# A recorded order from a table of ranks, and a dense layer that waits chunk by chunk

## Chip, cores, metric

One core of one Trainium2 chip. The metric is the device time of one execution in microseconds (us), lower is better. The profiled span, from the core's first to its last instruction, is some 1.7 us shorter than the device time; numbers called "span" are from the trace, the others are device times.

## What is computed

Two layers, each run twice: an attention with memory (32 heads of width 20, four segments of 512 rows) and a dense layer with relu, both on a normalised input with a residual. Cut to what matters:

```python
def _A_ref(x, wq, wk, wv, wo, beta):            # x: 1 x 2048 x 640, bf16
    ...                                          # q, k, v: 32 heads of 20, 4 segments of 512
    for s in range(N):
        logits = jnp.einsum('bhqd,bhkd->bhqk', qs, ks) * scale + mask     # causal inside a segment
        p = _softmax(logits, axis=-1)
        a_dot = jnp.einsum('bhqk,bhkd->bhqd', p, vs)
        num = jnp.einsum('bhld,bhde->bhle', pq, M)                        # read of the memory
        ...
        outs.append(g * a_mem + (1.0 - g) * a_dot)
        M = M + jnp.einsum('bhld,bhle->bhde', pk, vs)                     # write of the memory
        ...
    return o @ wo

def _B_ref(x, w1, w2):                           # 640 -> 1728 -> 640
    h = jnp.maximum(jnp.einsum('bsd,df->bsf', x, w1), 0)
    return jnp.einsum('bsf,fd->bsd', h, w2)

x = A_x
x = x + _A_ref(_layernorm(x), A_wq, A_wk, A_wv, A_wo, A_beta)
x = x + _B_ref(_layernorm(x), B_w1, B_w2)
x = x + _A_ref(_layernorm(x), A_wq, A_wk, A_wv, A_wo, A_beta)
x = x + _B_ref(_layernorm(x), B_w1, B_w2)
```

## The kernel before

The kernel is not written down in its final order. It is a set of generators (scores, products with the values, projections, normalisations, dense layers), each of which yields steps; a scheduler with a clock of its own (a guess of each step's duration) picks step after step and records it on its engine with the waits it needs. The hardware then runs each engine's instructions in that order. Which of several possible steps is recorded next:

```python
# Sched.run, cut: for each step that could be recorded now
b = self._best(op, None if st.first else resv)
end, start, k, rank = b            # rank: earliest start by the scheduler's own clock
key = (round(rank), op.due, st.serial)
if best is None or key < best[0]:
    best = (key, st, end, start, k)
```

`op.due` is the part that can be steered: without a table it comes from a rough pacing of the generators, and with one from `dues[key]`. Before, the table came out of 14 plans, each handing the next one the latest starts that would still end on time, and then 29 recorded random changes:

```python
for n in range(PLANS):              # 14
    P, S = plan(dues)
    end = max(S.t.values())
    new = justify(S)                # latest start of each step that keeps the end
    ...
end, P, S, dues = best
for seed in MOVES:                  # 29 seeds
    dues = shake(S, dues, seed)
    P, S = plan(dues)
```

The score rounds (L1286) write two double accumulator banks, X and Y, which two exponentials on ScalarE (L1300, L1297) empty; a triangular mask on Pool (L1276) follows. All other matmuls but the products with the values share three banks, MISC. The dense layer's first half makes 14 chunks of relu (13 of 128 features at L1586, a last one of 64 in another tile mode at L1598), the second half (L1616) sums over them:

```python
S.spawn(relu(NFULL, bk, tk), "relu")
w2t = yield Need("w2")
hr = []
for dc in range(NFULL + 1):         # all 14 chunks are asked for here
    th = yield Need("h", b, s, dc)
    hr.append(th)
for i in range(NJ):
    for hf in range(2):
        bk = None
        for dc in range(NFULL + 1):
            ...                      # fn: one 320-column matmul of chunk dc
            if dc == 0:
                _, bk = yield pe(mm_ns(320), lambda bank, fn=fn: [(lambda e: fn(e, bank), False)],
                                 (hr + w2t if i == hf == 0 else []), [MISC])
            else:
                tk = yield pe(mm_ns(320), lambda fn=fn, bank=bk.ap, dc=dc: [
                    (lambda e: fn(e, bank), dc == NFULL)])
```

The softmax here doesn't subtract the row's maximum and nothing guards it: scores larger than these inputs give would overflow.

## Time and profile before

| | before |
|---|---|
| device time, median (range) of 3 | 575.22 us (574.92 to 575.4) |
| span of the profile, granted TensorE clock | 573.2 us, 1.0 |
| first matmul; last matmul start to end | 1.25; 3.1 us |
| streaming of the matmuls | 500.5 us |
| 399 changes of tile mode | 38.6 us |
| small gaps, under 8 ns; 8 to 30 ns | 6.6; 6.5 us |
| stalls of 30 ns or more in the first 10 us | 3.5 us |
| later stalls: ahead of score rounds; relu ahead of the second half; all others | 3.76; 1.10; 8.30 us |

The page's busy share (97%) says that TensorE is the bound, but not how much an order could give. The table does: it is made from the start times of all matmuls, each gap between two starts minus the streaming time of the first. Only the last row, 13.2 us, is something that an order can take away, since it neither removes a matmul nor, as the prediction counts, a change of mode. The last row is sorted by the matmul that starts after the stall. Two matmul records are missing from this trace (5112 matmuls, 5114 weight loads).

### The profile page before, as it was taken

Reading aid. Unit: us, or ns where it says so; the run is one execution under the profiler, and the core shown is the slowest. Engines: PE = TensorE matmul, PEld = TensorE weight load, DVE = VectorE, ACT = ScalarE, POOL = GpSimd, SP = SyncE. Lnnn points to the kernel's source line nnn. Section 1 sums busy time; section 2 is a strip of 40 time slices with the busy share of each in tenths; the row PEclk is TensorE's granted clock in tenths of the full one; section 3 lists DMA queues with packets and bytes.
Section 4 is the critical chain, followed back from the end, with each engine's and each line's share of the span. In section 5 each row is a group of like instructions: output and inputs, shape, how many; then the busy total and the mean of one; then the engine's idle time right before and its main releaser. Section 6 shows DMA issues by size and latency. Waiting matters only on the chain.

```text
span 573.2 us, 12504 instructions
## 1 busy us (share of the span) xinstructions
PE 558.8 (97%) x5112; PEld 297.3 (52%) x5114; DVE 425.0 (74%) x1023; ACT 424.5 (74%) x517; POOL 213.3 (37%) x342
## 2 busy tenths in 40 slices
PE   8999989999999999999999999999999999999998
PEld 4454545444564444655446544455445644755655
DVE  6699989988999968976789683699756897624202
ACT  4899898989879978779998787896785887022140
POOL 3474546654444433444434441344331333002000
PEclk9999999999999999999999999999999999999999
DMA  6256777487354625545163720455315921522101
GB/s 217 94 126 137 148 137 150 145 217 108 66 79 71 94 43 87 95 74 106 31 123 58 115 50 15 71 97 89 66 19 69 160 55 19 92 64 44 50 0 47
DMA packets 126609, 50.62 MB, mean 88 GB/s; under 512 B 112120, under 2 KB 124600, under 8 KB 126552
## 3 DMA queue, kind: packets, MB, share of 16 engines
q1 hardware_dynamic: 124568, 42.19, 40.1%
q0 software_dynamic: 1552, 7.29, 4.3%
q8 instruction: 40, 0.66, 0.5%
q10 hardware_dynamic: 432, 0.34, 0.2%
q14 instruction: 17, 0.14, 0.1%
HBM read 15.16 MB, written 7.37 MB: 39 GB/s over the span
## 4 chain that ended last, share of the span: by engine, by line
PE 72%; DVE 20%; ACT 4%; DMA 2%; issue 1%; POOL 1%; SPq 0%; DVEq 0%
PE ps L1586 17%; PE ps L1616 17%; PE ps L947 12%; PE ps L1286 6%; PE ps L994 6%; PE ps L1532 5%; PE ps L1368 5%; ACT PT L1300 2%; DVE x_sb L1474 2%; DVE phq L1206 1%; DVE hT L1567 1%; DMA wv_r<-in_A_wv_dram 1%; DVE xn_tok L877 1%; DVE o_sb L1420 1%; DVE ktok L1142 1%; DVE stats L865 1%
## 5 line engine op out<-in xcount | busy, mean ns | idle before, releaser
L1300 ACT ACTIVATE PT<-ps 128x1024 bf16<-128x1024 f32 x256 | 248.2, 1024 | 38.5 <-PE ps L1286 37.7
L1276 POOL TENSOR_SCALAR_AFFINE_SELECT PT<-PT 128x512 bf16<-128x512 bf16 x256 | 171.0, 686 | 256.1 <-ACT PT L1300 220.5
L1616 PE MATMUL ps<-wb,hT 128*128 128x320 bf16 x896 | 133.7, 299 | 1.6 <-ACT hT L1568 1.0
L1586 PE MATMUL ps<-xnT,wb 128*128 128x512 bf16 x520 | 126.8, 380 | 1.0 <-DVE o_sb L1225 0.6
L1474 DVE TENSOR_TENSOR x_sb<-x_sb,ps 128x320 bf16<-128x320 bf16 x128 | 60.6, 478 | 68.5 <-PE ps L1616 54.8
L1616 PEld LDWEIGHTS ps<-wb,hT 128*128 128x128 bf16 x896 | 84.2, 98 | 38.7 <-issue 4.9
L1568 ACT ACTIVATE hT<-ps 128x512 bf16<-128x512 f32 (+1 forms) x64 | 36.8, 576 | 56.2 <-PE ps L1586 54.8
L1586 PEld LDWEIGHTS ps<-xnT,wb 128*128 128x128 bf16 x520 | 47.1, 98 | 56.5 <-issue 6.2
L1297 ACT ACTIVATE PT<-ps 128x1024 bf16<-128x1024 f32 x64 | 62.4, 1028 | 12.3 <-PE ps L1286 12.3
L994 PE MATMUL ps<-wv_r,xnT 128*128 128x320 bf16 x320 | 57.5, 300 | 1.1 <-DMA wv_r<-in_A_wv_dram 0.5
L947 PE MATMUL ps<-xnT,wq_p 128*128 128x512 bf16 x200 | 54.8, 380 | 0.4 <-DVE o_sb L1451 0.2
L947 PE MATMUL ps<-xnT,wk_p 128*128 128x512 bf16 x200 | 53.9, 380 | 0.0
L1532 PE MATMUL ps<-wo_r,oT 128*128 128x320 bf16 x280 | 47.4, 300 | 0.2 <-DVE x_sb L1474 0.2
L1368 PE MATMUL ps<-PT,va 128*32 128x128 bf16 (+3 forms) x896 | 40.7, 302 | 0.0
L994 PEld LDWEIGHTS ps<-wv_r,xnT 128*128 128x128 bf16 x320 | 29.4, 98 | 20.4 <-issue 3.7
L1286 PE MATMUL ps<-kq 20*128 20x512 bf16 (+3 forms) x560 | 35.3, 301 | 2.1 <-ACT PT L1300 2.0
L1567 DVE TENSOR_SCALAR hT<-ps 128x512 bf16<-128x512 f32 (+1 forms) x48 | 32.0, 672 | 4.6 <-PE ps L1586 4.3
L877 DVE TENSOR_SCALAR xn_tok<-x_sb,mv,rstd 128x640 bf16<-128x640 bf16 x64 | 32.8, 522 | 3.4 <-POOL rstd L873 2.2
L1532 PEld LDWEIGHTS ps<-wo_r,oT 128*128 128x128 bf16 x280 | 25.7, 98 | 15.7 <-issue 3.6
L864 DVE BATCH_NORM_STATS2 stats<-x_sb 128x6 f32<-128x320 bf16 x64 | 29.8, 465 | 1.5 <-DMA x_sb<-in_A_x_dram 1.3
L865 DVE BATCH_NORM_STATS2 stats<-x_sb 128x6 f32<-128x320 bf16 x64 | 30.2, 472 | 0.0
L1368 PEld LDWEIGHTS ps<-PT,va 128*32 128x32 bf16 x896 | 18.9, 96 | 21.5 <-issue 9.2
(111 smaller groups left out, 625.3 us busy)
## 6 DMA issues: line engine op xcount, KB each, us to landing
kq_scr<-kq SPq DMA_DIRECT2D x28, 120.0 KB
kqL<-kq_scr SPq DMA_DIRECT2D x28, 120.0 KB
out_dram<-x_sb SPq DMA_DIRECT2D x16, 160.0 KB, 1.9
wb<-in_B_w_dram POOLq DMA_DIRECT2D x5, 432.0 KB, 4.0
x_sb<-in_A_x_dram POOLq DMA_DIRECT2D x3, 640.0 KB, 4.7
wb<-in_B_w_dram POOLq DMA_DIRECT2D x2, 640.0 KB, 6.0
kq_away<-hT SPq DMA_DIRECT2D x5, 256.0 KB, 2.3
kq<-kq_away SPq DMA_DIRECT2D x5, 256.0 KB, 3.5
```

The source lines that it names most:

```text
L877: tn, bx = yield dve(D, 4, lambda e, a, t=t: e.tensor_scalar(a, x_sb[:, t, :], mv[:, t, 0:1], rstd[:, t:t + 1], ALU.subtract, ALU.mult), [ ...
L947: fn = lambda e, bank, k=k, w_p=w_p, c=c: e.matmul(bank, w_p[:, k, c * 128:(c + 1) * 128], xnT[:, k_, :, k, :], start=(k == 0), stop=(k == ...
L994: fn = lambda e, bank, k=k, i=i, hf=hf: e.matmul(bank[:, 0:320], xnT[:, k_, i, k, :], wv_r[:, k, hf * 320:(hf + 1) * 320], start=(k == 0), ...
L1276: tm = yield pool(590.0, lambda e: e.affine_select(out=reg, in_=reg, pattern=[[0, 4], [1, 128]], compare_op=ALU.is_ge, fill=0.0, base=0, c ...
L1286: fns.append((lambda e, x=x, j=j, hh=hh, N=N, o=o: e.matmul(ps[:, hh, o:o + N], kq(b, gg[x], 0)[32 * hh:32 * hh + DH, 128 * j:128 * j + 12 ...
L1297: fn = lambda e: e.activation(PT[:, :, 2 * k:2 * k + 2, 1024:1280], bs.ap.rearrange("p h (x t) -> p x h t", x=2), ACT.Exp, scale=SCALE)
L1300: fn = lambda e: e.activation(PT[:, items[0], 2 * k:2 * k + 2, c0:c0 + 512], bs.ap, ACT.Exp, scale=SCALE)
L1368: return [(lambda e, hh=hh, j=j: e.matmul(bank[32 * hh:32 * hh + 32, 128 * j:L], v_flat[b][:, (j * H + 8 * hh + g) * E1:(j * H + 8 * hh + ...
L1474: ta = yield dve(320, 1, lambda e: e.tensor_tensor(xa, xa, bk.ap[:, 0:320], ALU.add), [tk], early=HOT)
L1532: fn = lambda e, bank, k=k, hf=hf, o=ot.ap: e.matmul(bank[:, 0:320], o[:, k, :], wo_r[:, k, hf * 320:(hf + 1) * 320], start=(k == 0), stop ...
L1586: fn = lambda e, bank, k=k, dc=dc: e.matmul(bank, w1_r[:, k, dc * 128:(dc + 1) * 128], xnT[:, k_, :, k, :], start=(k == 0), stop=(k == FC ...
L1616: fn = lambda e, bank, dc=dc, q=q, h=h, hf=hf: e.matmul(bank[:, 0:320], h, w2_r[:, q, hf * 320:(hf + 1) * 320], start=(dc == 0), stop=(dc ...
```

## The change

Two things. The 14 plans and 29 changes are replaced by one plan without a table and one with a table of ranks, shipped in the file, that a search found. And the dense layer's second half asks for a chunk only at the matmul that reads it: the first matmul waits for chunk 0, the next for chunk 1, and so on. The intent: fewer stalls of TensorE at the same work.

```diff
-PLANS = 14
-MOVES = (100008, 100014, 100017, ... )
-def justify(S): ...
-def shake(S, dues, seed): ...
+def ranked(S):
+    keys = sorted((l[7] for l in S.log if l[7]), key=lambda k: [(isinstance(x, str), x) for x in k])
+    step = array.array("h", zlib.decompress(base64.b85decode("".join(TABLE.split()))))
+    assert len(step) == len(keys)
+    return dict(zip(keys, itertools.accumulate(step)))
+TABLE = """ ... """                 # cut: the packed ranks, one for each step
...
                 w2t = yield Need("w2")
-                hr = []
-                for dc in range(NFULL + 1):
-                    th = yield Need("h", b, s, dc)
-                    hr.append(th)
                 for i in range(NJ):
                     for hf in range(2):
                         bk = None
                         for dc in range(NFULL + 1):
+                            hr = []
+                            if i == hf == 0:
+                                th = yield Need("h", b, s, dc)
+                                hr = [th]
...
-                                                 (hr + w2t if i == hf == 0 else []), [MISC])
+                                                 hr + w2t, [MISC])
                             else:
                                 tk = yield pe(mm_ns(320), lambda fn=fn, bank=bk.ap, dc=dc: [
-                                    (lambda e: fn(e, bank), dc == NFULL)])
+                                    (lambda e: fn(e, bank), dc == NFULL)], hr)
...
-        (the loop over PLANS and MOVES)
+        P, S = plan(None)
+        P, S = plan(ranked(S))
```

Most lines of the new kernel stand six lines higher: scores L1280, dense layer L1580, L1592 and L1610.

## The prediction

> **What bounds the kernel now.** I read the page first (busy shares, slices), then the stretches of the span with the busy time of each engine, then the waits of TensorE alone, then the instructions in order of time around the longest of those waits.
>
> ```profile
> PE 558.8 (97%) x5112; PEld 297.3 (52%) x5114; DVE 425.0 (74%) x1023; ACT 424.5 (74%) x517; POOL 213.3 (37%) x342
> PEclk9999999999999999999999999999999999999999
> ```
>
> TensorE is busy 558.8 of the span's 573.2 us and is never throttled. That leaves 14.4 us of idle time in which no matmul is in flight; no other engine is near its limit over the whole span. But busy time counts the modelled ends of pipelined matmuls, so I took the span apart by the start times of the 5112 matmuls instead:
>
> - First matmul at 1.25 us.
> - Streaming: a 512-column matmul starts a median 216 ns before its successor on the same line, a 320-column one 136 ns. With columns divided by 2.4 GHz per matmul (four row- or column-tiles counted once, 55 ns for the 128-column transposes, 39 ns for the 84-column ones) all streaming comes to 500.5 us.
> - Changes of tile mode: the scores are recorded in row tiles of 20x128, the products with the values in column tiles of 128x32, the last chunk of the dense layer in 128x64, everything else in 128x128. A 320-column matmul followed by a score round takes 232 ns start to start instead of 136; a 512-column score round followed by a full matmul 317 ns instead of about 213. So one change costs about 97 ns, and there are 399: 38.6 us.
> - Small excess: gaps under 8 ns over the streaming time add to 6.6 us, and 485 gaps of 8 to 30 ns to 6.5 us (about 13 ns each, which I read as the price of a wait that is already satisfied plus the small fixed cost).
> - Stalls of 30 ns or more: 52, 16.7 us together, of which 3.5 us lie before 9.9 us (cold warm-up matmuls, first normalisation, landing of the value weights). So 13.15 us of stalls are left for an order to remove.
> - Last matmul start to end of span: 3.1 us.
>
> Sum: 1.25 + 500.5 + 38.6 + 13.1 + 16.7 + 3.1 = 573.2.
>
> ```profile
> 60.00:115.00 55.00, 51.38 (x545) 25.74 (x544) 49.88 (x126) 51.09 (x60) 32.28 (x50) 1.00 0.68 145
> 200.00:300.00 100.00, 99.96 (x974) 50.43 (x974) 77.54 (x170) 85.77 (x100) 41.09 (x63) 1.00 0.45 79
> 485.00:573.00 88.00, 84.45 (x566) 51.84 (x564) 29.15 (x74) 18.71 (x33) 5.67 (x12) 1.00 0.22 48
> ```
>
> Columns: length, busy TensorE, weight loads, VectorE, ScalarE, Pool. Between 60 and 115 us TensorE, VectorE (91%) and ScalarE (93%) are all nearly full, and TensorE loses 3.6 us there; from 200 to 300 us it loses almost nothing; in the last stretch it is alone.
>
> ```profile
> PE ps L1286 <- ACT PT L1300: 2.5, 4, 1.4
> ...
> PE ps L1616 <- ACT hT L1568: 1.0, 2, 0.5
> ...
> PE ps L1616 <- DVE x_sb L1474: 0.6, 1, 0.6
> ```
>
> This view names the waits of TensorE (total us, count, longest). First the scores waiting for the exponentials that free their two double banks; then the second half of the dense layer (L1616) waiting for the relu of the first half; then a bank of the three shared ones waiting for VectorE.
>
> ```profile
> 81.63 0.39 PE L1286 MATMUL ps<-kq 20*128 20x512 bf16 x4
> 81.95 0.77 PE L1443 MATMUL ps<-ident,oraw 128*128 128x128 bf16 x8
> 82.09 1.95 ACT L1300 ACTIVATE PT<-ps 128x1024 bf16<-128x1024 f32 x2
> 84.09 0.40 PE L1286 MATMUL ps<-kq 20*128 20x384 bf16 x8 [1.37 <-ACT PT L1300]
> ...
> 553.81 0.74 PE L1598 MATMUL ps<-xnT,wb 128*64 128x256 bf16 x10
> 553.91 1.05 ACT L1568 ACTIVATE hT<-ps 128x512 bf16<-128x512 f32 x2 [0.48 <-PE ps L1586]
> 555.02 2.02 PEld L1616 LDWEIGHTS ps<-wb,hT 128*128 128x128 bf16 x16 [0.75 <-ACT hT L1568]
> 555.02 2.21 PE L1616 MATMUL ps<-wb,hT 128*128 128x320 bf16 x15 [0.48 <-ACT hT L1568]
> ```
>
> The order put only eight small transposes (0.77 us) between two score rounds, while the two exponentials of a round need 1.95 us: a stall. And at 555.02 the first matmul of the dense layer's second half waits until all 14 chunks of relu are done, though it reads only the first.
>
> **What the Trainium skill says.** "TensorE: Matmul & The Clock Gate", section "Wait — 56ns, not 53.3ns?", gives N / 2.4 GHz plus about 2.5 ns start to start for a warm stream; the 216 and 136 ns here agree. "TensorEngine Tiling (Array Packing)", section "Key Properties", says that a change of tiling mode drains TensorE; it gives no figure, the trace has about 97 ns. The first page, section "The mechanism" of its Part 3, has matmuls in strict order, only weight loads moving ahead: so a matmul at the head of the queue that waits for the relu holds back every later one, as at 555.02, and the recorded order is what counts. "Trainium Kernel Development and Optimization", section "Performance Expectations", warns that matmul busy time is a bad measure because matmuls are pipelined; this is why I counted starts.
>
> **The change, part by part.** Both orders were compared instruction by instruction.
>
> (a) The work is the same: 5114 matmuls before, 5113 after (one filling matmul less at the start), the same count of every line, the same exponentials. A few copies out of the accumulators move between VectorE (1025 to 1022 instructions) and ScalarE (522 to 524). Streaming stays 500.5 us: 0.
>
> (b) Changes of tile mode: 399 before, 400 after. At 97 ns: +0.1 us. The 38.6 us stay. I had hoped the search would save here; it does not.
>
> (c) Waits recorded on TensorE: matmuls with a wait 679 before, 691 after. At 13 ns: +0.2 us.
>
> (d) Chunk-wise wait. In the last two dense layers, where nothing else can be put between, the order after is the same as before, except that the waits now stand before the 1st, 13th and 14th matmul of the second half. Twelve matmuls of 136 ns, 1.63 us, now cover what was a stall of 552 ns each. The last relu ends about 0.55 us after the last matmul that feeds it, so both stalls go fully: 2 x 0.55 = -1.1 us. In the six other layers other matmuls stood there already and no relu stall is in the trace: 0.
>
> (e) Score rounds. I added up streaming and mode changes between the starts of successive score rounds (160 rounds). A round needs about 2.35 us (81.63 to 84.09 with other ScalarE work in the queue is 2.46; two exponentials alone are 1.95 plus the round itself and its handover). Sum of what is missing to 2.35 us per gap: before 3.5 us, with gaps of 0.86, 1.80, 1.88 and 1.99 us between the 24th and 34th; after 0.9 us, none under 2.08. The stalls on exponentials in the trace (1440, 602, 494, 480, 244, 217 and 143 ns) add to 3.6 us. So -2.6 us. The last round moves from 460 to 469 us of TensorE work: rounds are spread out more, so ScalarE and VectorE have more room in the crowded stretches.
>
> (f) The three shared accumulator banks. I counted groups that start less than 0.9 us after the end of the group three before them: 20 before, 12 after; under 1.0 us between 60 and 110 us of work: 8 before, 4 after. Stalls put down to these banks and to other VectorE work are what remains: 13.15 - 3.6 - 1.1 = 8.4 us. The counts fall by 40 to 50%; since only the search's own timing, not the chip, guarded the order, I take a third: -2.8 us.
>
> (g) Start and end: the first value matmul waits for its weights from memory (at 9.86 us before) in both orders; the last add and store are the same: 0.
>
> Sum: +0.1 + 0.2 - 1.1 - 2.6 - 2.8 = -6.2 us, from 575.2 to about 569.0. All of it lies on the path, since TensorE is the bound. I shade it to 568.5, because an order found by search was presumably kept for being good in ways my three counts do not see.
>
> **Rivals.** (1) The stalls only move: TensorE waits at the new places for VectorE, which is 91 to 93% busy between 60 and 200 us and gets no less work. For it: the old order was itself the best of 14 plans and 29 random changes, and its remaining stalls are largely where the chip differs from the recording's timing, which a new table would not know. Then only (d) and some of (e) stay: 572 to 574 us. (2) The search removes nearly all stalls: 13.15 us less and nothing added gives 562 us, just over 2%. For it: 160 rounds with no tight gaps; against it, mode changes and base are untouched, and some stalls come from transposing transfers (0.4 us at 176.7) that the order hardly rules. (3) The order is bad on the chip, a long transfer or a transposition late somewhere in the queue that issues them, with TensorE idle for 3 us and more: 580 us. Against it: DMA is at 68% at most in any of the stretches after 10 us, and SyncE has the same 217 instructions.
>
> **Range and chances.** A floor is 562 (no stall after 9.9 us); going more than 2% faster needs 563.7, so 11.5 of the 13.15 us. A ceiling with all gains lost is 575 to 576. Eight in ten: 564.5 to 572.5. Faster by over 2%: 0.06; within 2%: 0.92; slower: 0.02.
>
> **What would show it.** After: TensorE busy about 558 with idle time down from 14.4 to about 8 us; no wait of the second half (now L1610) on the relu, and the second half of the last two layers starting within 0.1 us of the chunk before it; scores waiting for exponentials under 1 us in total; 400 mode changes at the same 97 ns. I would be wrong if a mode change costs differently in another neighbourhood, if TensorE's waits for VectorE grow between 60 and 200 us, or if the first value matmul starts later than 9.9 us.

## The result, and the profile after

570.64 us (median of 4 runs, 569.9 to 571.42) against 575.12 us for the kernel before (4 runs, 574.92 to 575.4). The ratio is 0.9922, 95% interval 0.9905 to 0.9939: 0.8% faster, within 2%. All four runs of the new kernel were at clock 1.0. Ratios here and below are the mean time of one kernel's fast runs over that of the other's fast runs of the same rounds, so not quite the ratio of the medians quoted.

The busy line of the new kernel's page, and the first of the three stretches shown of before (length, then busy TensorE, weight loads, VectorE, ScalarE, Pool, then clock, DMA share, GB/s):

```profile
PE 558.4 (98%) x5113; PEld 296.0 (52%) x5113; DVE 425.8 (75%) x1020; ACT 424.5 (75%) x519; POOL 215.4 (38%) x343
```

```profile
60.00:115.00 55.00, 53.94 (x568) 26.33 (x569) 52.24 (x130) 51.24 (x62) 31.52 (x51) 1.00 0.80 165
```

TensorE's idle time fell from 14.4 to 10.8 us (569.2 minus 558.4), not to 8. In the crowded stretch from 60 to 115 us TensorE loses 1.1 us where it lost 3.6, with 23 more matmuls placed there, although VectorE (95%, before 91%) and ScalarE (93%) are no emptier than before. TensorE's waits in the new kernel (total us, count, longest), those of the warm-up cut:

```profile
PE ps L1526 <- DMA oT<-o_sb: 1.1, 1, 1.1
PE ps L1610 <- DVE x_sb L1468: 1.0, 2, 0.5
PE ps L1280 <- ACT PT L1291: 0.7, 2, 0.5
...
PE ps L1280 <- ACT PT L1294: 0.3, 1, 0.3
```

The relu is gone from this list, and the scores wait 1.0 us for exponentials instead of 3.6. What leads now is one transpose by DMA (`oT`), and banks that VectorE frees late. The place of the prediction's last quoted lines, now in the new kernel (start us, us, engine, line):

```profile
550.28 0.74 PE L1592 MATMUL ps<-xnT,wb 128*64 128x256 bf16 x10
550.39 1.05 ACT L1562 ACTIVATE hT<-ps 128x512 bf16<-128x512 f32 x2 [0.48 <-PE ps L1580]
...
550.95 2.56 PEld L1610 LDWEIGHTS ps<-wb,hT 128*128 128x128 bf16 x20 [0.20 <-issue]
550.95 2.75 PE L1610 MATMUL ps<-wb,hT 128*128 128x320 bf16 x19
```

The second half starts at 550.95, while the last relus (550.39 to 551.44) still run.

All runs taken apart in the same way as the table of before (streaming is 500.2 to 501.8 us in all of them, and the small gaps are within 0.2 us of those of before, in split_apply 0.4; the time of the mode changes is their number times 96.7 ns):

| kernel | span | mode changes: n, us | first 10 us | ahead of score rounds | relu, second half | all others | the last three |
|---|---|---|---|---|---|---|---|
| before | 573.24 | 399, 38.6 | 3.51 | 3.76 | 1.10 | 8.30 | 13.16 |
| new | 569.17 | 400, 38.7 | 3.44 | 1.56 | 0 | 7.09 | 8.65 |
| new_again (same kernel) | 569.07 | 400, 38.7 | 3.64 | 1.54 | 0 | 7.40 | 8.95 |
| chunk_only | 572.39 | 399, 38.6 | 3.19 | 3.72 | 0 | 8.83 | 12.54 |
| order_only | 572.06 | 400, 38.7 | 3.33 | 1.56 | 4.55 | 6.21 | 12.33 |
| split_apply | 576.84 | 444, 42.9 | 3.08 | 1.14 | 0 | 11.59 | 12.73 |
| tight_rounds | 575.91 | 407, 39.4 | 3.15 | 7.92 | 0 | 7.65 | 15.56 |
| tiny_mask_old | 566.64 | 399, 38.6 | 3.15 | 4.51 | 1.10 | 1.39 | 7.00 |
| tiny_mask_new | 562.56 | 400, 38.7 | 3.18 | 1.57 | 0 | 1.49 | 3.05 |
| swap_oT | 567.75 | 400, 38.7 | 3.29 | 1.55 | 0 | 6.47 | 8.02 |
| port_clock_a | 580.60 | 398, 38.5 | 3.16 | 7.76 | 0 | 13.56 | 21.32 |
| port_clock_b | 579.16 | 402, 38.9 | 2.92 | 7.78 | 0 | 10.61 | 18.39 |
| port_clock_c | 571.30 | 399, 38.6 | 2.33 | 1.66 | 0 | 9.53 | 11.19 |

The span is 4.1 us shorter and the last column 4.5. The difference is the missing records: new has all its 5113 matmuls and port_clock_c all of its own, but before, chunk_only and tiny_mask_old lack two each (0.47 us of false stalls under "all others") and the other traces three (0.65 to 0.69 us). Without the false stalls "all others" is 7.8 us in before, 7.1 in new and 6.7 in the repeat, and the last column falls from 12.7 to 8.65: the whole gain of span is there.

### The profile page after: what moved, and what is told of

It reads as the page before. It is cut to its first block, busy times and chain, and to the rows that moved or that the text cites. A ratio compares the mean times of both kernels' runs of the same rounds, so it can differ in the third digit from the quotient of the medians.

```text
span 569.2 us, 12508 instructions
## 1 busy us (share of the span) xinstructions
PE 558.4 (98%) x5113; PEld 296.0 (52%) x5113; DVE 425.8 (75%) x1020; ACT 424.5 (75%) x519; POOL 215.4 (38%) x343
## 4 chain that ended last, share of the span: by engine, by line
PE 79%; DVE 12%; ACT 4%; DMA 3%; POOL 1%; issue 1%
PE ps L1610 18%; PE ps L1580 17%; PE ps L941 12%; PE ps L1280 7%; PE ps L1526 7%; PE ps L988 7%; PE ps L1362 6%; ACT PT L1294 2%; DMA oT<-o_sb 2%; DVE xn_tok L871 1%; DVE stats L858 1%; DVE x_sb L1468 1%; DVE stats L859 1%; PE ps L1143 1%; PE ps L1230 1%; DVE ktok L1136 1%
## 5 line engine op out<-in xcount | busy, mean ns | idle before, releaser
L1610 PE MATMUL ps<-wb,hT 128*128 128x320 bf16 x896 | 136.2, 299 | 1.0 <-DVE x_sb L1468 1.0
L1580 PE MATMUL ps<-xnT,wb 128*128 128x512 bf16 x520 | 126.8, 380 | 0.2 <-DVE hT L1561 0.2
L1610 PEld LDWEIGHTS ps<-wb,hT 128*128 128x128 bf16 x896 | 83.2, 98 | 39.3 <-issue 7.6
L1580 PEld LDWEIGHTS ps<-xnT,wb 128*128 128x128 bf16 x520 | 48.0, 98 | 57.8 <-issue 7.0
L1291 ACT ACTIVATE PT<-ps 128x1024 bf16<-128x1024 f32 x64 | 62.5, 1032 | 14.4 <-PE ps L1280 14.1
L941 PE MATMUL ps<-xnT,wq_p 128*128 128x512 bf16 x200 | 57.3, 380 | 0.3 <-DVE o_sb L1219 0.3
L941 PE MATMUL ps<-xnT,wk_p 128*128 128x512 bf16 x200 | 56.0, 380 | 0.0
L1526 PE MATMUL ps<-wo_r,oT 128*128 128x320 bf16 x280 | 51.8, 299 | 1.2 <-DMA oT<-o_sb 1.1
L928 DVE CAST kq<-ps 128x512 bf16<-128x512 f32 x45 | 30.8, 685 | 11.1 <-PE ps L941 10.7
L1561 DVE TENSOR_SCALAR hT<-ps 128x512 bf16<-128x512 f32 (+1 forms) x50 | 33.2, 666 | 7.1 <-PE ps L1580 6.9
L871 DVE TENSOR_SCALAR xn_tok<-x_sb,mv,rstd 128x640 bf16<-128x640 bf16 x64 | 33.3, 529 | 4.1 <-POOL rstd L867 2.7
L1280 PE MATMUL ps<-kq 20*128 20x512 bf16 (+3 forms) x560 | 35.3, 301 | 0.2
L858 DVE BATCH_NORM_STATS2 stats<-x_sb 128x6 f32<-128x320 bf16 x64 | 29.5, 465 | 1.8 <-DMA x_sb<-in_A_x_dram 1.5
```

What stands on the lines that cost most here:

```text
L871: tn, bx = yield dve(D, 4, lambda e, a, t=t: e.tensor_scalar(a, x_sb[:, t, :], mv[:, t, 0:1], rstd[:, t:t + 1], ALU.subtract, ALU.mult), [ ...
L941: fn = lambda e, bank, k=k, w_p=w_p, c=c: e.matmul(bank, w_p[:, k, c * 128:(c + 1) * 128], xnT[:, k_, :, k, :], start=(k == 0), stop=(k == ...
L1280: fns.append((lambda e, x=x, j=j, hh=hh, N=N, o=o: e.matmul(ps[:, hh, o:o + N], kq(b, gg[x], 0)[32 * hh:32 * hh + DH, 128 * j:128 * j + 12 ...
L1291: fn = lambda e: e.activation(PT[:, :, 2 * k:2 * k + 2, 1024:1280], bs.ap.rearrange("p h (x t) -> p x h t", x=2), ACT.Exp, scale=SCALE)
L1526: fn = lambda e, bank, k=k, hf=hf, o=ot.ap: e.matmul(bank[:, 0:320], o[:, k, :], wo_r[:, k, hf * 320:(hf + 1) * 320], start=(k == 0), stop ...
L1580: fn = lambda e, bank, k=k, dc=dc: e.matmul(bank, w1_r[:, k, dc * 128:(dc + 1) * 128], xnT[:, k_, :, k, :], start=(k == 0), stop=(k == FC ...
```

## The experiments

In the experiments the order of every step and the engine of every movable copy is frozen in a table, so that an edit changes one thing and the scheduler rearranges nothing in answer. Frozen copies of the two orders were first compared with their originals and were the same instruction for instruction. The edit that all of them share:

```diff
-                    y.due = self.dues[y.key]
+                    y.due, want = self.dues[y.key]
+                    y.alts = [a for a in y.alts if a[0] == want] or y.alts
...
-                key = (round(rank), op.due, st.serial)
+                key = (op.due, 0, st.serial) if self.dues else (round(rank), op.due, st.serial)
```

Runs of one batch share a chip and the runs of the kernel before; its medians were 576.15, 575.26, 575.4 and 575.24 us in the four batches. Compare ratios across batches, not times. The first batch (chunk_only, order_only, tight_rounds, split_apply) needs care: six of its eleven runs of the kernel before had a mean granted clock of 0.997 and took 576.15 to 577.01 us, while the five at 1.0 took 574.35 to 575.10 (median 575.01). All runs of the four experiments had 1.0, so their ratios, taken over all eleven, make them look some 0.2% better than they are.

### Which part does it: chunk_only and order_only

chunk_only is the old order with the new waits; order_only is the new order with the old waits:

```diff
 # chunk_only: the table holds the order of before; in the dense layer as in the change
+                            if i == hf == 0:
+                                th = yield Need("h", b, s, dc)
+                                hr = [th]
 # order_only: the table holds the new order; in the dense layer as before
+                for dc in range(NFULL + 1):
+                    th = yield Need("h", b, s, dc)
+                    hr.append(th)
```

> The old order, instruction for instruction, with the chunk-wise wait alone. Theory (the wait is worth what the trace of before shows at the last two dense layers, 2 x 0.55 us, and elsewhere nothing): 1.1 us under before, about 574.0 us, and no gap over 0.1 us ahead of the second half of the last two layers. Rival A (the new wait was the main part of the 4.5 us): 571.5 us or less. Rival B (the stall only moves to the 13th or 14th matmul): same as before, 575.1, with a gap of 0.3 us or more there.

> The new order on every engine, with the old single wait for all 14 chunks. Theory (order and wait add up; order is worth about 3.4 us, the wait 1.1 us or a little more because the new order also starts two earlier second halves right behind their last chunk): 571.7 to 572.5 us. Rival (the two parts need each other, the order alone is worth little): 574 us or more.

Measured: chunk_only 574.39 us (573.81 to 574.61), ratio 0.9973 (0.9954 to 0.9991); order_only 574.28 us (573.51 to 574.79), ratio 0.997 (0.9953 to 0.9987). Against the five runs of before at the same clock, 1.0, each part alone is worth 0.6 to 0.7 us by the medians, and 0.9 and 1.2 us by the spans of the profiles: 0.1 to 0.2%, not the 0.3% of the ratios. Together they are worth 4.5 us, 0.8%. My expectation for the order alone was too good, and the rival that the parts need each other was right.

The trace says why. The old order always had other matmuls between the last chunk of the first half and the second half, except in the last two layers. The new order does not: there the second half stands right behind its last chunk in five of the eight layers (three earlier ones and the last two; I had counted two earlier ones). TensorE's timeline in order_only and TensorE's longest waits there:

```profile
223.35 0.74 PE L1576 MATMUL ps<-xnT,wb 128*64 128x256 bf16 x10
225.73 1.53 PE L1594 MATMUL ps<-wb,hT 128*128 128x320 bf16 x10 [1.65 <-ACT hT L1546]
```

```profile
PE ps L1594 <- ACT hT L1546: 2.6, 3, 1.6
PE ps L1594 <- DVE hT L1545: 1.6, 2, 1.0
```

and the same place in the new kernel, where the relus of the last chunks run beside the matmuls of the first ones:

```profile
223.90 0.74 PE L1592 MATMUL ps<-xnT,wb 128*64 128x256 bf16 x10
224.57 1.53 PE L1610 MATMUL ps<-wb,hT 128*128 128x320 bf16 x10
```

The five stalls of order_only are 1.72, 1.04, 0.69, 0.55 and 0.55 us, 4.55 us together. So the chunk-wise wait removes 1.1 us of stalls on the old order and 4.55 us on the new one. Of this, 3.45 us is a hole that the new order opens and only the chunk-wise wait closes: presumably because its search, which had the chunk-wise wait, was free to let the two halves meet (the search itself was not at hand to test). The same order takes away 2.2 us of score stalls and, in the profile of the new kernel, 0.7 us of others (1.2 by the table, with the false stalls).

### What a score round needs: tight_rounds

In the new order, 16 score rounds are recorded earlier, ahead of 1.22 to 1.30 us of full matmuls which before stood in front of them. The mode changes stay nearly the same (407). Schematic, one of 16 places in TensorE's sequence:

```diff
+score round (8 matmuls, 20x128)
 full matmuls, 1.22 to 1.30 us of streaming
-score round (8 matmuls, 20x128)
```

> The new order with 16 score rounds between 35 and 80% of the recording pulled ahead of 1.2 us of full matmuls on TensorE; the other engines' orders are untouched. What is missing to a spacing of 2.46 us rises from 1.4 to 8.2 us (2.35 us: from 0.9 to 6.7), and 7 more mode changes cost 0.7 us. Theory (a short gap before a round stalls TensorE by what is missing, and the longer gap after it gives nothing back): 6 to 7.5 us over the new kernel, 576.5 to 578 us, with the stalls put down to the exponentials. Rival (ScalarE or the bank hand-over was not the limit, or TensorE catches up later): under 2 us more, 572.5 us or less.

Measured: 577.58 us (577.05 to 579.36), ratio 1.0033 (1.0014 to 1.0052). The stalls ahead of score rounds go from 1.56 to 7.92 us:

```profile
PE ps L1264 <- ACT PT L1275: 3.6, 6, 0.8
PE ps L1264 <- ACT PT L1278: 3.2, 5, 0.9
```

Eight of the moved rounds stall for 0.63 to 0.94 us, and every one of them starts 2.424 to 2.430 us after the round ahead of it. So the least distance of two rounds is 2.425 us, a little over the 2.35 us that the prediction used, and what TensorE has recorded between two rounds must fill it. The mechanism of the prediction's step (e) is shown: closer rounds cost what is missing, here 6.4 us.

### What a change of tile mode costs: split_apply

If a mode change really costs 97 ns, the 400 that both orders keep are worth 38.7 us. In the new order, 45 groups of products with the values (column tiles) are moved behind the next two full matmuls. That adds 44 changes. Schematic, one of 45 places:

```diff
-16 products with the values (128x32)
 full matmul (128x128)
 full matmul (128x128)
+16 products with the values (128x32)
 full matmuls ...
```

> The new order with 44 more changes of tile mode on TensorE (444 instead of 400): 45 groups of value products that stood directly behind a score round now follow two more full matmuls. Nothing else moves on any engine. Theory (every change costs about 97 ns on the path): 44 x 0.097 = 4.3 us over the new kernel, about 574.9 us. Rival (the drain hides in waits or in the slack before the next round): under 1.5 us more, 572 us or less.

Measured: 578.67 us (578.11 to 578.88), ratio 1.0047 (1.003 to 1.0064); the span is 7.7 us longer than the new kernel's. The trace has 444 changes. The table prices them by their number, but the gaps can be read directly: the 59 changes from a full matmul to value products (15 in the new kernel) have a median of 96 ns over streaming, the 154 from a score round to a full matmul (110 in the new kernel) one of 105 ns (113 in the new kernel), and of this some 10 ns are the four tiles of a round starting 3 to 4 ns one after the other. So 44 more at 97 ns are some 4.2 us. The other 3.4 us are stalls that the move brought, such as one of 1.5 us ahead of an output projection that waits for a transpose. That the move of the groups brought them by releasing something later is argued, not shown. So the price holds in places it was not measured at. The total is more than that price, so an edit of the order is never the price of its mode changes alone.

### What the stalls that stayed are: tiny_mask_old and tiny_mask_new

"All others" fell by 1.2 us where I had predicted 2.8. The trace of the new kernel shows VectorE instructions of one form with two durations. Around 67 us (start us, us, engine, line):

```profile
66.66 1.30 POOL L1270 TENSOR_SCALAR_AFFINE_SELECT PT<-PT 128x512 bf16<-128x512 bf16 x2
66.71 1.42 DVE L871 TENSOR_SCALAR xn_tok<-x_sb,mv,rstd 128x640 bf16<-128x640 bf16 x2
...
68.05 1.27 DVE L928 CAST kq<-ps 128x512 bf16<-128x512 f32 x2
...
68.79 0.33 PE L1230 MATMUL ps<-BD,phq 128*128 128x84 bf16 x4 [0.40 <-DVE kq L928]
```

Two normalisations (L871) begin 0.05 us after a mask on Pool and take 1.42 us instead of 0.86; the casts queued behind them end late, and a matmul of the memory read waits 0.40 us for the last of these. The Trainium skill, page "SBUF — State Buffer", section "Who interferes with whom", says that VectorE and Pool share a pair of ports under an exclusive lock, and that VectorE needs it for instructions with two SBUF inputs and in its two-port modes. The trace agrees: summed over each form's excess over its own fast duration, VectorE loses 23.0 us before and 20.9 us after, nearly all of it beside a Pool instruction, and none in reads of accumulators or in the statistics of the normalisation.

To see what that costs TensorE, both orders were run with masks of 4 columns instead of 4 x 128. The result is wrong: the masks no longer cover the triangle (the comparison with the reference passed all the same). The instructions, their order and their waits stay.

```diff
-                    reg = PT[:, x, :, PT_OFF[j]:PT_OFF[j] + 128]
+                    reg = PT[:, x, 0:1, PT_OFF[j]:PT_OFF[j] + 4]
...
-                        out=reg, in_=reg, pattern=[[0, 4], [1, 128]], ...
+                        out=reg, in_=reg, pattern=[[0, 1], [1, 4]], ...
```

> The new kernel's instructions unchanged on every engine (the order written out in full instead of found from ranks), as the base for this batch and for the interval. Every theory: 570.6 us, ratio 0.992 to the kernel before.

> Wrong result on purpose. The old kernel's order, with every causal mask on Pool cut from 512 to 4 elements per partition. Theory (VectorE instructions with two SBUF inputs or a fast mode stand still while a Pool mask runs: 23 us of such delay in the trace of before; part of it reaches TensorE through late accumulator banks): VectorE's excess falls under 3 us, stalls of TensorE after 10 us fall from 13.2 to 10 or 11 us, time 2 to 3.5 us under before, 572 to 573 us. Rival (the delayed VectorE work has slack): same as before within 1 us.

> Wrong result on purpose. The same cut in the new kernel. Theory (the new order lost part of its gain to delays of VectorE that the recording does not know; without them the gain comes to what the recording's own clock shows, 6.6 us): stalls of TensorE after 10 us fall from 8.6 to 4 or 5 us, time 4 to 5 us under the new kernel, 566 to 567 us, and 6 to 7 us under the old kernel with the same cut. Rival (the shortfall has other causes, above all late transposes by DMA such as the 1.26 us at 390.8): the difference between old and new stays 4 to 5 us.

Measured: new_again 570.51 us (569.98 to 570.8), ratio 0.9917 (0.9904 to 0.9931); tiny_mask_old 568.72 us (568.38 to 569.06), 0.9888 (0.9875 to 0.9902); tiny_mask_new 564.58 us (564.3 to 565.14), 0.9818 (0.9804 to 0.9831). With tiny masks VectorE's excess falls to 0.2 us (old order) and 0.1 us (new). The normalisation's group (busy us, mean ns, idle before by releaser) in the new kernel and with tiny masks:

```profile
L871 DVE TENSOR_SCALAR xn_tok<-x_sb,mv,rstd 128x640 bf16<-128x640 bf16 x64 | 33.3, 529 | 4.1 <-POOL rstd L867 2.7 <-DMA xnT<-xn_tok 0.5 <-PE ps L835 0.5
```

```profile
L855 DVE TENSOR_SCALAR xn_tok<-x_sb,mv,rstd 128x640 bf16<-128x640 bf16 x64 | 27.2, 435 | 1.9 <-POOL rstd L851 1.0 <-PE ps L819 0.5 <-DMA xnT<-xn_tok 0.3
```

and TensorE's waits in tiny_mask_new after the warm-up, where only a third one of 0.3 us follows:

```profile
PE ps L1264 <- ACT PT L1275: 0.7, 2, 0.5
PE ps L1510 <- DMA oT<-o_sb: 0.5, 1, 0.5
```

"All others" drops from 8.30 to 1.39 us in the old order and from 7.09 to 1.49 in the new one: about four fifths of that class goes with the full masks (nearly nine tenths without the false stalls: 7.8 to 0.9 and 7.1 to 0.8). The late stalls of TensorE that the trace puts down to VectorE fall from 6.97 to 0.78 us and from 5.50 to 0.17. The time falls by 6.5 us (575.26 to 568.72) and 5.9 us (570.51 to 564.58). But my own theory fell here. I had thought that the new order lost its missing 1.6 us specially to the masks, so that without them it would be 6 to 7 us ahead. It stays 4.1 us ahead (568.72 to 564.58), not much less than with full masks (4.75). The delays cost both orders about the same, and the reordering hardly touches them: the scheduler's clock has no such lock, so presumably no order was chosen for it. One caution: tiny masks are also done sooner (230 ns a mask instead of 687), which frees Pool and hands their tile on earlier, so not all of the 5.9 us need be the lock: in the two lines of the normalisation above, VectorE's wait for Pool's `rstd` falls from 4.1 to 1.9 us. No late stall of TensorE is put down to Pool itself, with full masks or tiny ones, and VectorE's excess goes from 20.9 to 0.1 us, so the lock is likely to be most of it, but no run separates the two.

### One late transpose: swap_oT

The longest single stall after the warm-up in the new kernel lies at 390.8 us. SyncE's queue of transposes and TensorE's start there:

```profile
386.16 1.40 SPq L1117 DMA_TRANSPOSE ktok<-kq  x1
387.61 1.28 SPq L1516 DMA_TRANSPOSE oT<-o_sb  x1
```

```profile
390.81 0.58 PE L1526 MATMUL ps<-wo_r,oT 128*128 128x320 bf16 x3 [1.10 <-DMA oT<-o_sb]
```

swap_oT exchanges these two in the queue and nothing else:

```diff
+oT<-o_sb      transpose, needed at once by the output projection
 ktok<-kq      transpose, not urgent
-oT<-o_sb
```

> The new kernel with two neighbouring DMA transposes exchanged in SyncE's queue: the one for the attention output that TensorE waits 1.26 us for at 390.8 us goes ahead of one for the memory keys. Theory (the transfer was late only because it stood behind the other, 1.4 us, in the queue): the 1.26 us stall shrinks to under 0.3 us, span 0.8 to 1.3 us shorter, about 569.5 us. Rival (it waited for its buffer or its input): the stall stays over 1 us, or an equal one appears within the next 15 us.

Measured: 569.72 us (569.48 to 570.7), ratio 0.9909 (0.9895 to 0.9923), against 570.51 for the new kernel in the same batch. The stall went from 1.26 us by start times (0.98 in the repeat's profile) to 0.69, not to zero, because the transpose now just ahead of it held the queue for 2.10 us in this run (1.31 in the new kernel), so that `oT` was issued at 386.99, only 0.6 us earlier than at 387.61:

```profile
384.85 2.10 SPq L1445 DMA_TRANSPOSE otok<-oraw  x1
```

The direction fits, but the intervals overlap: inconclusive. Single stalls vary from run to run; one in the new kernel at 82 us, put down to VectorE, was 0.43 us in one profile and 1.14 in the other.

### Can a search that knows of the lock do better: port_clock_a, port_clock_b, port_clock_c

The recording clock was given the lock (a VectorE step with two SBUF inputs or in a fast mode waits while a mask is running) and a random search over the ranks, some 7,000 to 12,000 plans each, started from the new table. For a and b I also shortened the clock's guess of the transposes to what short ones take in the trace. For c I left those guesses alone.

```diff
 # recording clock, schematic
+if e == "dve" and step uses the shared ports:
+    start = max(start, end of the mask that holds them)     # the choice sees this wait
 # a and b only
-transposes: issue and landing as in the kernel, 4000 ns more while weights load
+transposes: 1230 ns issue, 900 ns landing, 1000 ns more while weights load
```

> The new kernel's instructions and waits in another order (398 mode changes). It was searched with a recording clock that makes a VectorE instruction with two SBUF inputs or a fast mode wait while a Pool mask runs, lets the recording take other work first, and has transfer times set from the trace. On that clock the new kernel's order ends at 564.8 us and this one at 560.0. Theory (the stalls left in the new kernel come mostly from those delays and an order that knows them avoids them): VectorE's excess falls from 20.9 to under 12 us, stalls of TensorE after 10 us from 8.6 to 4 or 5 us, time 565.5 to 567 us, ratio to before 0.983 to 0.986. Rival (the delays fall anew wherever the order puts the masks, because the real timing drifts from the clock's): 569.5 us or more.

> A second order from the same search with another seed; on its clock it ends at 561.2 us. Theory: 566.5 to 568.5 us, a little behind the first, excess of VectorE under 12 us. Rival: 569.5 us or more.

> The new kernel's instructions unchanged, as the base of this batch. Every theory: about 570.5 us, ratio 0.992.

> A third searched order (399 mode changes). The two before it failed because I had also shortened the recorded transfer times; here the transfer times are the new kernel's own, and the clock differs from it in the waits of VectorE for Pool masks (and a few durations of TensorE and VectorE) alone. On this clock the old order ends at 569.8, the new one at 565.7 and this one at 562.2 us; VectorE's delays are 15.2, 16.0 and 6.1 us. Theory (knowing the delays is what was missing): VectorE's excess 8 to 12 us instead of 20.9, stalls of TensorE after 10 us 5 to 7 us, time 567 to 569 us, ratio to before 0.986 to 0.989. Rival (real timing drifts too far from any such clock): excess over 15 us and 570 us or more.

Measured: port_clock_a 582.34 us (580.47 to 583.81), ratio 1.0121 (1.0102 to 1.014); port_clock_b 580.02 us (578.17 to 585.77), 1.0094 (1.0055 to 1.0133); new_third, the new kernel again in the same batch, 570.42 us (0.9913, 0.9901 to 0.9926; one execution of 581.33 at clock 0.949); port_clock_c 572.59 us (569.63 to 573.34), 0.994 (0.9918 to 0.9962). a and b are clearly slower than the new kernel. c is slower by its median, but the intervals of the two ratios overlap: its two runs at clock 0.999 and 1.0 took 569.63 and 570.76 us, like the new kernel, and its four at 0.997 took 572.38 to 573.34. The times of the rivals came true each time; the largest waits, though, were for transposes, not for masks.

In a, one transpose explains much: SyncE and ScalarE, then TensorE:

```profile
86.98 6.16 SPq L1101 DMA_TRANSPOSE ktok<-kq  x1
...
101.53 1.06 ACT L1117 ACTIVATE etmp<-ktok 128x1024 bf16<-128x1024 bf16 x1 [5.66 <-DMA ktok<-kq]
```

```profile
104.47 0.61 PE L1264 MATMUL ps<-kq 20*128 20x384 bf16 x8 [5.63 <-ACT PT L1278]
105.01 0.61 PE L925 MATMUL ps<-xnT,wq_p 128*128 128x512 bf16 x1
```

The transpose at 86.98 landed 14.5 us after its issue (9.5 us for its counterpart in the new kernel). The search, told that such a transfer is quick, had put its reader early into ScalarE's queue. Behind it the score exponentials stood still (ScalarE idle for 5.66 us), and TensorE with them (5.63 us). In b the same reader waits 6.74 us at 101.92, and TensorE 6.7. Then, in a, for some 5 us, 512-column matmuls started some 430 ns apart instead of 216 and the one at 105.01 shows 0.61 us where 0.39 is usual: half clock. The columns are those of the stretches above; the third number from the right is the granted clock:

```profile
103.00:109.70 6.70, 5.23 (x38) 1.72 (x38) 2.86 (x6) 3.95 (x5) 4.17 (x6) 0.50 0.42 108
```

The Trainium skill, "TensorE: Matmul & The Clock Gate", section "What's actually happening", has the clock fall to half after an idle window of about 3.4 us; 5.63 us of idling fits. In c a wait of 2.4 us was followed by some 13 matmuls that were about 134 ns longer each, twice as long for 320 columns, so here a gap shorter than that window was enough. TensorE was busy for 1.02 of the 3.4 us up to the fall of the clock:

```profile
PE ps L1509 <- DMA oT<-o_sb: 2.4, 1, 2.4
```

```profile
438.80:442.20 3.40, 1.02 (x14) 0.41 (x12) 1.53 (x5) 2.03 (x3) 1.36 (x3) 1.00 1.20 105
442.30:445.60 3.30, 3.30 (x14) 1.84 (x13) 1.76 (x5) 0.00 (x0) 0.64 (x2) 0.50 1.13 146
```

Some 3.4 us at half clock in 571 lower the mean clock by 0.3%. By this estimate c's other runs at 0.997, and those of the kernel before, had one such stretch too; their traces were not kept, so what brought it on there is open.

VectorE's excess in a, b and c is 15.9, 15.8 and 17.2 us: the search did avoid part of the lock (20.9 in the new kernel), but I had expected 8 to 12 of c. A search of the same effort on the kernel's own, unchanged clock found nothing better than the new table (no run shows this). Why an order that is better by a better clock does not become better on the chip is partly settled. In all three the longest wait of TensorE comes from a late transpose, in a and b by way of ScalarE, and half clock follows. "All others" in the table holds the slow matmuls as well, and in c that wait. Without the slow matmuls and the false stalls it is about 10.8 us in a and 8.1 in b, against 7.1 in the new kernel; these stalls were not traced one by one. In c, without its wait of 2.45 us by start times too, it is 5.4: there the search did save stalls, and one late transpose with the half clock after it took the gain back.

No version that was run clearly beats the new kernel with a right result.

## Why the prediction was right or wrong

Predicted 568.5 us, 564.5 to 572.5; measured 570.64. The gain was 4.5 us where the sum of the steps said 6.2.

- **Base and (a).** Right. Streaming is unchanged (500.5, 500.9; 500.2 in the repeat, apart by missing records alone), and the same matmuls run. The 13.15 us of stalls that the prediction took for removable hold 0.47 us of false ones from the two missing records.
- **(b) Mode changes.** Right: 399 to 400, and split_apply shows about the same price in new places.
- **(c) Waits at 13 ns.** The size was wrong, with no weight in the sum. Gaps of 8 to 30 ns do not go with waits. In the old kernel 285 of the 485 follow a group of four row or column tiles, which start 3 to 4 ns one after the other while the sum counts them as one; eight follow a pair of column tiles, and one is at a change of mode. Of the 191 left, between full matmuls, 172 are at matmuls without a wait and 19 at matmuls with one; among the gaps under 8 ns a satisfied wait adds about 0.3 ns (2.4 against 2.1 ns over streaming). What the 191 are, some 12.7 ns each, stays open.
- **(d) Chunk-wise wait.** -1.1 us for the last two layers: right, the trace has 1.10 before and 0 after, in chunk_only too. "In the six other layers ... 0" is true only of the old order. In the new order the same edit carries 4.55 us, as order_only shows. The prediction treated the two parts as a sum; they are not one.
- **(e) Score rounds.** -2.6 us predicted; the stalls ahead of score rounds fell from 3.76 to 1.56, so -2.2. Right in mechanism (tight_rounds) and nearly in size; the need of a round is 2.425 us, not 2.35. By the wait view the scores wait 1.0 us, at the edge of the "under 1 us" that I named.
- **(f) Shared banks.** This is the step that failed in size: -2.8 us predicted, -1.2 measured (8.30 to 7.09), -0.9 in the repeat, and -0.7 and -1.1 without the false stalls. I had taken the remaining class for a matter of how closely groups follow on three banks, and scaled it by my counts of close groups (20 to 12). The tiny masks show that four fifths and more of it goes with the full masks, mostly as VectorE held up beside them, which both orders suffer alike and which no count of banks sees. The sum is 1.7 us short by the device times (6.2 against 4.5) and 2.1 by the spans: (f) lacks 1.7 to 2.1 us and (e) 0.4, and (c), counted at +0.2, did not come.
- **(g) Start and end.** Right: the first 10 us hold 3.51 and 3.44 us of stalls, and the last matmul's start to the end 3.1 in both.
- **The shade from 569.0 to 568.5** for unknown virtues of a searched order was wrong in sign.
- **Rivals.** That stalls only move (572 to 574) is refuted for the whole change, but order_only (574.28 us beside 575.01 of before at the same clock) shows that this is just what the table does without its partner. Between 60 and 200 us the rival held for the whole change too: the stalls put down to VectorE are 3.7 us before, 3.6 after and 4.3 in the repeat. The gain lies in score rounds, relu and the rest of the span. That nearly all stalls vanish (562) needs the delays by masks away: tiny_mask_new has 3.05 us of stalls left and 564.58 us. The bad order (580) did not happen here, but port_clock_a shows at 582.34 that it was a real way to go.

## What to carry to other kernels

Two edits found together should be measured apart and together: here either one alone gave 0.1 to 0.2%, and the pair 0.8%, because the order opens a hole that only the finer wait closes. When stalls name an engine that is not full, look first for instructions of one form with two durations and for what runs beside the long ones; most of a mis-sized "bank" stall was VectorE slowed beside Pool's masks. An order found on a model clock is only as good as that clock's worst guess: a transfer that it takes for quick can cost more than hundreds of well-placed steps win.

## What the Trainium skill lacked or had wrong

- "TensorEngine Tiling (Array Packing)" says that a change of tiling mode drains TensorE, without a figure. Here one costs about 97 ns (medians of 96 ns into column tiles and 105 ns out of a score round in split_apply).
- "TensorE: Matmul & The Clock Gate" has the clock fall after an idle window of about 3.4 us. In port_clock_c about 13 matmuls ran at half speed after TensorE had idled for 2.4 us and been busy for 1.0 of the 3.4 us before the fall.
- "SBUF — State Buffer" describes the lock between VectorE and Pool rightly, but not what it costs a kernel bound by TensorE: 20.9 us of VectorE time, and up to 5.9 us of 570.5 in the end time, gone with masks of 4 columns (which also free Pool sooner).
- No page that I read gives the price of a wait that is already satisfied at a matmul (about 0.3 ns here), or explains the 191 gaps of some 12.7 ns that TensorE makes between full matmuls, mostly without one.
- "DMA: Bandwidth & Descriptors" gives bandwidths and rules for transposes, but not how late a small one lands behind others: 9.5 us after issue for one in the new kernel, 14.5 us for its counterpart in port_clock_a.
